# Attention and mixer kernel: scores with each head's q and k on its own half of the rows, and one group of four blocks in every other chunk transposed by DMA

## The chip, the cores and the metric

The kernel runs on one core of a Trainium2 chip. The metric is device time in microseconds (us). A core has TensorE (PE in the profile; PEld is its weight load), VectorE (DVE), ScalarE (ACT), GpSimd (POOL) and SyncE (SP). DMAs are issued from the queues of SP and ACT here.

## The reference, cut to what matters

Batch 4, 8 heads, 576 positions, head dimension 64, all in float32.

```python
scores = scale * np.matmul(q, k.transpose(0, 1, 3, 2))
...
h = np.maximum(x @ w1 + b1, 0.0)          # x: psi_rel / psi_i, 32 hidden
bias = h @ w2
scores = scores + bias.transpose(2, 0, 1)[None, :, :, :]
scores = scores - np.max(scores, axis=-1, keepdims=True)
attn = np.exp(scores)
attn = attn / (np.sum(attn, axis=-1, keepdims=True) + 1e-09)
return np.matmul(attn, v)
```

The result, reshaped to (4, 576, 512), goes through a mixer: a token step `u = x + (relu(x^T w_tok1) w_tok2)^T` and a channel step `u + relu(u w_ch1) w_ch2`.

## The kernel before

The work has three stages that overlap at their borders.

**Bias.** 36 blocks build the 8 x 576 x 576 bias. For each, ACT and DVE make four rectified tiles (lines 422 and 424), TensorE multiplies them with w2 into one of two PSUM tiles called `pair` (line 440, 16 instructions), `over` (line 446) scales them into one of four `eb` buffers, and `put` stores the buffer in DRAM (line 451, SP queue). Beside that, SP loads v once for its size (`sums`, line 465, eight loads) and the weights for their sizes (`meas`, line 303).

**Units.** A unit is one pair of heads of one batch entry; there are 16. It loads kT and qT (line 620, ACT queue) as tiles of 128 rows: rows 0 to 63 hold head dimensions for the two heads side by side (1152 columns), rows 64 to 127 hold the same again. A unit has five chunks of query rows, four of 128 and a last one of 64 rows per head that handles both heads at once. For each chunk:

- `scores` (line 653) multiplies q and k. In chunks 0 to 3 it is one step per head: two matrix products of 288 columns, one on rows 0 to 63 and one on rows 64 to 127, into the two banks of one `pair` tile. In the last chunk it is four products of 320 columns, two from each half of the rows, into the upper and the lower half of the partitions of one `pair` tile. A float32 product is two instructions in the profile.
- `biased` (line 657, DVE) adds the bias, takes the row maximum and writes the tile z; `top` (676 or 678) and `numer` (671, ACT) make the exponential in place.
- `flip` (line 690, TensorE) transposes groups of four blocks of 128 columns of z into a PSUM bank; `flip_hi` (693, ACT) and `flip_lo` (697, DVE) split them into two float16 parts in a `t2a` tile. FLIPS says how many groups each chunk turns this way: two in chunks 0 to 3, one in the last.
- The rest of z's columns, 128 of them in every chunk, is split into two float16 parts in a `p2` tile by `hi` (line 307) and `lo` (line 322, POOL) and transposed by DMA on the SP queue (`turn`, line 709) into one of two `t2` tiles.
- `back` (lines 733 to 735) multiplies the transposed attention with v in 30 products; the norm, the token mixer (783 to 785, 792 to 794) and a store follow at the end of a unit.

**Channel step.** Lines 955 to 957 and 985 to 987, with the decoding of its weights (lines 544 to 559) beside the units.

**Order.** Nothing is left to queues to decide: every step has a cost, a due time from the tables DUE, TICK and BASE, an engine choice from ON, and buffers that it takes and frees. `Plan.order` writes one fixed order of instructions per engine from these. A `scores` step of a head takes one of the two `pair` tiles and frees it after `biased`; a `turn` takes one of two `t2` tiles, which is free again after the `back` two chunks earlier. A DMA step on the SP queue is `D`, on the ACT queue `Q`, a DMA transposition on SP `X`.

Of the kernel before, what the change touches and what calls it, by code (L numbers as in the profile page):

```python
# [8 lines left out]
F32 = mybir.dt.float32  # L9
# [12 lines left out]
NF = 32  # L22
TAB = 1148
# [12 lines left out]
TICK = 2.39  # L36
BASE = 61.71
# [7 lines left out]
ON = {'top': {'V': (0.15, 0.74), 'A': (0.22, 0.08)},  # L45
      'dlo': {'V': (0.67, -2.69), 'P': (1.78, -2.0)},
      'norm': {'V': (0.35, -23.09), 'A': (0.88, 14.02)},
      'rect': {'A': 0.68, 'V': (0.45, -13.36)},
      'over': {'A': 0.65, 'V': (0.72, 6.22)},
      'vh': {'P': (0.7, -10.93), 'V': (0.4, 2.41), 'A': (0.6, -8.52)},  # L50
      'vl': {'P': (1.36, 16.26)},
      'hi': {'A': (1.05, -14.51), 'V': (0.67, 19.73)},
      'lo': {'P': (2.32, 8.15)}}
DUE = {'blk': 32.56,
       'blkn': 0.64,
       'rect': -60.12,
       'bmm': -130.42,
       'over': -7.68,
       'put': -27.47,
       'bl': -14.28,  # L60
       'bln': 15.14,
       'sums': -75.84,
       'sumsn': 0.81,
       'meas': -57.01,
       'measn': -1.94,
       'measw': 95.9,
       'measwn': 5.09,
       'amax': 57.87,
       'scales': 29.14,
       'scalet': -69.14,  # L70
       'scalec': -164.62,
       'fill': 232.3,
       'fill1': 251.05,
       'tok': 91.96,
       'tokn': 1.42,
       'dec1': 41.92,
       'dec2': -0.99,
       'dec3': -43.49,
       'dec4': 30.17,
       'dec5': 2.45,  # L80
       'load_k': -31.58,
       'load_q': 67.25,
       'load_v': -142.39,
       'prep_k': -55.55,
       'prep_kl': -22.13,
       'prep_q': 79.74,
       'prep_ql': 14.53,
       'prep_v': -118.61,
       'prep_vh': -0.88,
       'prep_vl': 145.08,  # L90
       'scores': 30.55,
       'biased': 82.97,
       'top': -4.71,
       'exp': -22.34,
       'hi': -110.65,
       'lo': -17.61,
       'flip': 33.53,
       'fliphi': 28.08,
       'flip2': 1.68,
       'fliplo': 9.58,  # L100
       'turn': -6.91,
       'back': -21.64,
       'norm': 85.56,
# [1003 lines left out]
```

## Time and profile before

| | |
|---|---|
| median of 3 runs | 718.59 us (713.29 to 719.01) |
| profiled execution | 719.23 us, of which the span is 717.4 us |
| mean granted TensorE clock over the span | 0.982 |
| PE busy | 663.8 us, 93% |
| DVE busy | 464.0 us, 65% |
| ACT busy | 377.4 us, 53% |
| POOL busy | 166.6 us, 23% |

The shares are means over stages with different limits, so the stages are read one by one. Busy times overlap: a matrix product's row lasts until its modelled end, while the next has already begun, so what a step costs TensorE is read from its start to the start of the next step. A queue's own rows (ACTq, SPq) are issues and waits, not computation.

### The profile page before, as it was taken

What the parts mean: (1) busy time and instruction counts of PE and PEld (TensorE: products, weight loads), DVE (VectorE), ACT (ScalarE), POOL (GpSimd) and SP (SyncE); (2) the same over time, 40 slices, a digit from 0 to 9 for tenths busy, and PEclk for the clock granted to TensorE, in tenths of its full rate; (3) what the DMA queues carried; (4) which work ended last, traced back from release to release, by engine and by line L of the source; (5) the groups of instructions that cost most, each with busy time, mean ns of one, the idle gap of its engine ahead of it and who ended that gap; (6) DMA issues with size and microseconds to landing.
All of it is one profiled execution on the core that took longest, in us unless ns stands there. A gap on an engine that the chain in (4) does not pass through costs nothing.

```text
span 717.4 us, 16724 instructions
## 1 busy us (share of the span) xinstructions
PE 663.8 (93%) x6612; PEld 396.6 (55%) x6612; DVE 464.0 (65%) x1122; ACT 377.4 (53%) x767; POOL 166.6 (23%) x228
## 2 busy tenths in 40 slices
PE   2775879999999999999979999999999999999997
PEld 1422346766767766777757676544444444446443
DVE  4598978987889998887887878479971022112110
ACT  1585878765877888867865853335531022012010
POOL 0102125232546543533322110003450000000000
PEclk9899999999999999999998999999999999999999
DMA  9978778897665586343552127967733120020021
GB/s 341 341 261 268 252 244 255 231 257 227 199 170 147 172 246 207 101 139 113 136 99 69 24 67 222 255 209 192 194 85 118 58 59 1 11 78 31 14 87 33
DMA packets 86815, 111.43 MB, mean 155 GB/s; under 512 B 46928, under 2 KB 56400, under 8 KB 86736
## 3 DMA queue, kind: packets, MB, share of 16 engines
q1 hardware_dynamic: 77232, 81.52, 39.3%
q10 hardware_dynamic: 9504, 28.84, 12.8%
q8 instruction: 52, 0.85, 0.5%
q14 instruction: 27, 0.22, 0.1%
HBM read 80.31 MB, written 20.05 MB: 140 GB/s over the span
## 4 chain that ended last, share of the span: by engine, by line
PE 74%; DVE 7%; DMA 7%; ACT 5%; issue 3%; POOL 2%; ACTq 0%; SPq 0%; POOLq 0%; DVEq 0%
PE pair L653 9%; PE bank L690 8%; PE bank L955 7%; PE bank L956 7%; PE bank L957 7%; PE bank L987 7%; PE bank L985 6%; PE bank L986 6%; PE bank L733 3%; DMA slots<-v 3%; PE pair L440 3%; PE bank L735 3%; PE bank L734 2%; DVE z L657 2%; DVE t2a L697 2%
## 5 line engine op out<-in xcount | busy, mean ns | idle before, releaser
L653 PE MATMUL pair<-kk,qq 64*128 64x288 f32 (+1 forms) x640 | 107.9, 458 | 8.0 <-DVE mx L657 5.0
L657 DVE CUSTOM_DVE_ANT_0 z<-pair,slots 128x576 f32<-128x576 f32 x144 | 108.0, 756 | 10.1 <-PE pair L653 9.5
L671 ACT ACTIVATE z<-z,mx 128x576 f32<-128x576 f32 x144 | 110.8, 774 | 5.8 <-POOL vl L322 1.9
L697 DVE TENSOR_TENSOR t2a<-bank,t2a 128x512 f16<-128x512 f32 x144 | 98.2, 686 | 21.5 <-ACT t2a L693 20.8
L693 ACT ACTIVATE t2a<-bank 128x512 f16<-128x512 f32 x144 | 84.5, 587 | 46.4 <-PE bank L690 41.9
L690 PE MATMUL bank<-id,z 128*128 128x128 f32 x576 | 95.4, 290 | 4.9 <-ACT z L671 4.8
L690 PEld LDWEIGHTS bank<-id,z 128*128 128x128 f32 x576 | 62.0, 143 | 36.8 <-issue 12.1
L996 DVE SCALAR_TENSOR_TENSOR o<-bank,crow,ur 128x512 f32<-128x512 f32 x18 | 13.5, 751 | 106.1 <-PE bank L987 106.1
L733 PE MATMUL bank<-vh,t2a 128*128 128x65 f16 (+1 forms) x704 | 76.9, 198 | 0.3 <-DVE x L767 0.2
L734 PE MATMUL bank<-vl,t2a 128*128 128x64 f16 (+1 forms) x704 | 76.2, 194 | 0.0
L733 PEld LDWEIGHTS <-t2a 128*128 128x128 f16 (+1 forms) x704 | 65.8, 100 | 18.6 <-issue 12.6
L735 PE MATMUL bank<-vh,t2a 128*128 128x65 f16 (+1 forms) x704 | 75.8, 195 | 0.0
L955 PE MATMUL bank<-slots 128*128 128x384 f16 (+1 forms) x192 | 67.8, 353 | 0.0
L956 PE MATMUL bank<-slots 128*128 128x384 f16 (+1 forms) x192 | 67.7, 353 | 0.0
L957 PE MATMUL bank<-slots 128*128 128x384 f16 (+1 forms) x192 | 67.7, 353 | 0.0
L734 PEld LDWEIGHTS <-t2a 128*128 128x128 f16 (+1 forms) x704 | 66.6, 102 | 0.5 <-issue 0.2
L735 PEld LDWEIGHTS <-t2a 128*128 128x128 f16 (+1 forms) x704 | 66.7, 101 | 0.0
L322 POOL TENSOR_TENSOR p<-z,p 128x128 f16<-128x128 f32 x80 | 35.4, 444 | 131.7 <-ACT p L307 109.0
L653 PEld LDWEIGHTS pair<-kk,qq 64*128 64x128 f32 (+1 forms) x640 | 43.4, 177 | 35.1 <-issue 14.4
L424 DVE TENSOR_SCALAR slots<-slots 128x576 f32<-128x576 f32 x108 | 53.1, 562 | 14.4 <-PE pair L440 14.3
L440 PE MATMUL pair<-slots 128*32 128x288 f32 x576 | 47.6, 448 | 14.6 <-ACT slots L446 14.2
L977 ACT ACTIVATE ur<-ur,sc 128x512 f32<-128x512 f32 x18 | 12.9, 719 | 83.1 <-DMA ur<-um 68.7
(173 smaller groups left out, 1410.4 us busy)
## 6 DMA issues: line engine op xcount, KB each, us to landing
raw<-wc SPq DMA_DIRECT2D x48, 512.0 KB, 4.3
bd<-slots SPq DMA_DIRECT2D x36, 288.0 KB, 3.6
kk<-kT ACTq DMA_DIRECT2D x16, 576.0 KB, 5.1
qq<-qT ACTq DMA_DIRECT2D x16, 576.0 KB, 6.2
slots<-bd SPq DMA_DIRECT2D x16, 576.0 KB, 4.7
tv<-v ACTq DMA_DIRECT2D x16, 320.0 KB, 3.8
slots<-v SPq DMA_DIRECT2D x8, 640.0 KB, 13.0
um<-x SPq DMA_DIRECT2D x16, 256.0 KB, 3.5
```

The costliest lines, as they stand in the source:

```text
L653: PE.matmul(out=o[:, n, 0:i], lhsT=qq[w, q0:q0 + m], rhs=kk[w, k0:k0 + i], start=True, stop=True)
L657: V.tensor_tensor_reduce(out=st["z"][z.i][:, o].rearrange("p (n j) -> p n j", n=2), in0=pairs[ph.i][:, :, 0:i], in1=(bias_m[hp][:, c, h, : ...
L671: A.activation(out=zz, in_=zz, func=ACTF.Exp, bias=mx_t[z.i][:, 2 + h:3 + h], scale=0.125)
L690: PE.transpose(banks[tb.i][:, n * 128:(n + 1) * 128], st["z"][z.i][:, 512 * i + n * 128:512 * i + (n + 1) * 128], id32)
L693: A.activation(out=st["t2a"][h.i][:, 0:4].rearrange("p n q -> p (n q)"), in_=banks[tb.i], func=ACTF.Copy)
L697: V.tensor_tensor(out=x[:, 512:1024], in0=banks[tb.i], in1=x[:, 0:512], op=ALU.subtract)
L733: PE.matmul(out=o, lhsT=lh, rhs=vh[:, n, 0:D + 1], start=(i == 0), stop=False)
L734: PE.matmul(out=ps[q, h, 0:D], lhsT=lh, rhs=vl[:, n, :], start=False, stop=False)
L735: PE.matmul(out=o, lhsT=ll, rhs=vh[:, n, 0:D + 1], start=False, stop=(i == 4))
L955: PE.matmul(out=ps[:, 0:n], lhsT=w[0][:, c], rhs=uh[:, c], start=(c == 0), stop=False)
L956: PE.matmul(out=ps[:, 0:n], lhsT=w[0][:, c], rhs=ul[:, c], start=False, stop=False)
L957: PE.matmul(out=ps[:, 0:n], lhsT=w[1][:, c], rhs=uh[:, c], start=False, stop=(c == 3))
```

## The change

q and k are laid out so that a head has rows of its own: head 0 on rows 0 to 63, head 1 on rows 64 to 127, each 576 columns. A load has half the bytes. `scores` is one step for both heads in chunks 0 to 3, four products of 288 columns that alternate between the halves of the rows, and it takes both `pair` tiles at once. In the last chunk each head multiplies from its own half, into its own half of the partitions, six products of 320, 256, 256, 320, 64 and 64 columns.

FLIPS goes from 22221 to 12121 per unit: chunks 0 and 2 turn one group by TensorE, and their DMA transposition has 640 columns in place of 128 (times two for the parts).

`put` goes from SP's queue to ACT's. Three kinds of loads are held back until a given `over` step is done: the later `sums` loads, the `meas` loads, and kT and qT of every unit but the first. The planner can hand out two buffers of one kind to a step. All numbers of DUE, ON, TICK and BASE are new, so the order on every engine is a new one.

```diff
+GATES = (4, 6, 14)
...
-TICK = 2.39
-BASE = 61.71
+TICK = 2.23
+BASE = 67.32
...
-FLIPS = "22221" * 16
+FLIPS = "12121" * 16
...
-QUEUE = {'put': 'D', 'bias': 'D', 'k': 'Q', 'q': 'Q', 'v': 'Q', 'out': 'D', 'ur': 'Q', 'sums': 'D', 'w2': 'D'}
...
+QUEUE = {'put': 'Q', 'bias': 'D', 'k': 'Q', 'q': 'Q', 'v': 'Q', 'out': 'D', 'ur': 'Q', 'sums': 'D', 'w2': 'D'}
...
                     for h in s.take:
-                        if not room[h.kind]:
+                        n = sum(o.kind == h.kind for o in s.take)
+                        if len(room[h.kind]) < n:
                             break
-                        t = max(t, min(room[h.kind])[0])
+                        t = max(t, sorted(room[h.kind])[n - 1][0])
...
-            st["kk"][i] = p.tile([128, PW], F32, name=f"kk{i}")
-            st["qq"][i] = p.tile([128, PW], F32, name=f"qq{i}")
+            st["kk"][i] = p.tile([128, S], F32, name=f"kk{i}")
+            st["qq"][i] = p.tile([128, S], F32, name=f"qq{i}")
...
+        def hold_back(s, n):
+
+            overs[n].next.append(s)
+            s.left += 1
+
+        for x, i in late:
+            if i >= GATES[0]:
+                hold_back(x, (i - GATES[0]) // 2)
...
-            x = add(wire("meas", 1.67 * n / 512), t, lambda e, h=h, w=w, n=n: load_words(e, st["raw"][h.i], w, n), take=[h])
+            x = add(wire("meas", 1.67 * n / 512), t, lambda e, h=h, w=w, n=n: load_words(e, st["raw"][h.i], w, n), after=[overs[GATES[1]]], take=[h])
...
-            lk = add(wire("k", 1.84), t0 + DUE["load_k"], load("kk", hk, kT), take=[hk])
-            lq = add(wire("q", 1.84), t0 + DUE["load_q"], load("qq", hq, qT), take=[hq])
+            early = [overs[min(GATES[2] * u, 35)]] if u else []
+            lk = add(wire("k", 1.0), t0 + DUE["load_k"], load("kk", hk, kT), after=early, take=[hk])
+            lq = add(wire("q", 1.0), t0 + DUE["load_q"], load("qq", hq, qT), after=early, take=[hq])
...
+                phs = [Hold("pair") for _ in range(2 if c < NCH else 1)]
+
+                def scores(e, c=c, phs=phs):
+
+                    kk, qq = st["kk"][hk.i], st["qq"][hq.i]
+                    if c < NCH:
+                        job = [(h, pairs[phs[h].i][:, n, 0:288], c * 128, 128, n * 288, 288) for n in range(2) for h in range(2)]
+                    else:
+                        ps = pairs[phs[0].i]
+                        job = [(0, ps[0:64, 0, 0:320], 512, 64, 0, 320), (1, ps[64:128, 0, 64:320], 512, 64, 0, 256),
+                               (0, ps[0:64, 1, 0:256], 512, 64, 320, 256), (1, ps[64:128, 1, 0:320], 512, 64, 256, 320),
+                               (0, ps[0:64, 1, 256:320], 512, 64, 512, 64), (1, ps[64:128, 0, 0:64], 512, 64, 0, 64)]
+                    for h, o, q0, m, k0, n in job:
+                        w = slice(64 * h, 64 * h + 64)
+                        PE.matmul(out=o, lhsT=qq[w, q0:q0 + m], rhs=kk[w, k0:k0 + n], start=True, stop=True)
+
+                lead = chain("scores", add({"T": 1.12 if c < NCH else 0.8}, t + DUE["scores"], scores, after=[*ready, *bias_in[hp, c]], take=[*phs, z], free=[hk, hq]))
+                for h, ph in enumerate(phs):
...
-                    s = add({"V": 0.68 if c < NCH else 0.75}, t + DUE["biased"], biased, after=[s, *tops], free=[ph])
+                    s = add({"V": 0.68 if c < NCH else 0.75}, t + DUE["biased"], biased, after=[lead, *tops], free=[ph])
...
-        return np.tile(x.reshape(NB, HP, 2, S, D).transpose(1, 0, 4, 2, 3).reshape(HP * NB, D, PW), (1, 2, 1))
+        return x.reshape(NB, HP, 2, S, D).transpose(1, 0, 2, 4, 3).reshape(HP * NB, 2 * D, S)
```

## Rows read from the trace of the kernel before

**Rows 1.** The profile's page, its part 1 (busy time, share of the span) and part 4 (the chain of work that ended last, by engine).

```profile
PE 663.8 (93%) x6612; PEld 396.6 (55%) x6612; DVE 464.0 (65%) x1122; ACT 377.4 (53%) x767; POOL 166.6 (23%) x228
...
PE 74%; DVE 7%; DMA 7%; ACT 5%; issue 3%; POOL 2%; ACTq 0%; SPq 0%; POOLq 0%; DVEq 0%
```

**Rows 2.** Busy time by stretch: the stretch in us, its length, then busy us and instructions of PE, PEld, DVE, ACT and POOL, the granted TensorE clock, the share of DMA, GB/s.

```profile
0.00:32.00 32.00, 15.71 (x179) 8.95 (x179) 14.62 (x41) 10.12 (x14) 2.08 (x16) 0.95 0.94 356
32.00:100.00 68.00, 49.74 (x569) 22.03 (x570) 58.87 (x134) 52.08 (x86) 13.59 (x16) 0.95 0.78 259
100.00:180.00 80.00, 74.15 (x991) 52.65 (x988) 67.74 (x178) 56.06 (x130) 25.85 (x41) 0.96 0.85 241
180.00:440.00 260.00, 252.45 (x3551) 183.88 (x3548) 218.59 (x557) 194.12 (x434) 99.80 (x132) 0.99 0.51 138
440.00:717.00 277.00, 271.79 (x1336) 129.14 (x1334) 104.14 (x215) 64.98 (x108) 25.24 (x24) 1.00 0.35 98
```

**Rows 3.** TensorE in order of time, 205.9 to 213 us: start, duration, line, operation. L653 is scores, L690 a flip, L733 to L735 a back.

```profile
205.90 0.66 PE L690 MATMUL bank<-id,z 128*128 128x128 f32 x4
206.49 0.77 PE L653 MATMUL pair<-kk,qq 64*64 64x320 f32 x8
207.19 0.66 PE L690 MATMUL bank<-id,z 128*128 128x128 f32 x4
207.68 0.19 PE L733 MATMUL bank<-vh,t2a 128*128 128x65 f16 x1
...
208.59 0.63 PE L690 MATMUL bank<-id,z 128*128 128x128 f32 x4
209.16 1.24 PE L653 MATMUL pair<-kk,qq 64*128 64x288 f32 x8
210.33 0.66 PE L690 MATMUL bank<-id,z 128*128 128x128 f32 x4
...
211.73 0.63 PE L690 MATMUL bank<-id,z 128*128 128x128 f32 x4
212.30 0.76 PE L653 MATMUL pair<-kk,qq 64*128 64x288 f32 x4
212.98 0.65 PE L690 MATMUL bank<-id,z 128*128 128x128 f32 x4
```

**Rows 4.** One line's instructions: all score products, and the token mixer's first line of its second part (ten instructions a unit): duration in ns least, median and most, then the starts of the first and the last.

```profile
L653 PE MATMUL pair<-kk,qq x640: 402/430/846, 52.7 to 420.3; 64*128 64x288 f32 x128, 64*64 64x320 f32 x32
...
L792 PE MATMUL bank<-hh,wt2h x160: 218/219/245, 131.6 to 442.6; 128*128 128x128 f16 x128, 128*64 128x128 f16 x32
```

**Rows 5.** Groups of instructions by line and shape: count, busy us, mean ns of one, idle time of the engine before them and what ended it.

```profile
L697 DVE TENSOR_TENSOR t2a<-bank,t2a 128x512 f16<-128x512 f32 x144 | 98.2, 686 | 21.5 <-ACT t2a L693 20.8
L657 DVE CUSTOM_DVE_ANT_0 z<-pair,slots 128x576 f32<-128x576 f32 x128 | 95.2, 748 | 8.5 <-PE pair L653 7.9
L693 ACT ACTIVATE t2a<-bank 128x512 f16<-128x512 f32 x144 | 84.5, 587 | 46.4 <-PE bank L690 41.9 <-DVE m L297 2.7 <-PE pair L653 1.1
L322 POOL TENSOR_TENSOR p<-z,p 128x128 f16<-128x128 f32 x80 | 35.4, 444 | 131.7 <-ACT p L307 109.0 <-ACT mx L676 16.7 <-DVE t2a L697 2.4
L307 ACT ACTIVATE p<-z 128x128 f16<-128x128 f32 x80 | 24.1, 303 | 2.6 <-POOL vl L322 2.1 <-ACT z L671 0.2
L322 POOL TENSOR_TENSOR xl<-x,xh 128x640 f16<-128x640 f32 x16 | 22.4, 1403 | 18.8 <-ACT xh L307 17.0 <-DVE mx L657 1.7
L307 ACT ACTIVATE xh<-x 128x640 f16<-128x640 f32 x16 | 11.7, 728 | 1.7 <-DVE x L767 1.6
```

**Rows 6.** Waits over the whole span: engine and line, what it waited for, us in total, times, the longest.

```profile
PEld pair L653 <- DVE mx L657: 10.9, 21, 3.8
...
PE pair L653 <- DVE mx L657: 5.0, 5, 3.6
```

**Rows 7.** DMA transpositions on the SP queue: L709 are the turns of z (two blocks of 128 columns each), L930 those of the channel step (four blocks). For each the issue (ns least, median, most), and the time to landing; the idle time of TensorE that ended with a turn; the wait of the SP queue for a free `t2` tile.

```profile
L709 SPq DMA_TRANSPOSE t<-p x80: 1167/1183/3247, 74.5 to 424.5; - x80
...
DMA to landing us min/median/max: 2.3/3.5/7.3
...
  DMA t<-p: 3.8, 4
...
L930 SPq DMA_TRANSPOSE slots<-slots x14: 1189/1216/1262, 358.6 to 449.6; - x14
...
DMA to landing us min/median/max: 2.4/2.5/6.4
...
SPq L709 <- PE bank L735: 74.0, 44, 6.2
```

**Rows 8.** The ACT queue and the SP queue at the start, in order of time: start, duration, queue, line, what is issued; in brackets the idle time before and what ended it.

```profile
2.12 14.26 SPq L465 DMA_DIRECT2D slots<-v  x8
...
9.73 7.58 ACTq L620 DMA_DIRECT2D qq<-qT  x3
17.42 0.77 ACT L422 ACTIVATE slots<-slots 128x576 f32<-128x576 f32 x1 [9.42 <-DMA kk<-kT]
...
31.55 1.45 ACT L446 ACTIVATE slots<-pair,slots 128x576 f32<-128x576 f32 x2 [4.42 <-DMA bd<-slots]
...
51.52 0.33 ACTq L624 DMA_DIRECT2D tv<-v  x1
```

More of the change, by code (lines that the diff above doesn't have):

```diff
@@ L54 @@
[L54 to L103, printed above, removed]
-       'mix0': -81.74,
-       'mix1': 47.34,
-       'relu': -93.88,
-       'mix2': -76.85,
-       'mix2b': -112.19,
-       'store': 54.71,
-       'w1': 37.13,
-       'w1n': 10.89,
-       'U0': -31.54,
-       'U0n': -5.32,
-       'U1n': -19.8,
-       'U1': -24.21,
-       'U2': 119.12,
-       'Un': 2.81,
-       'U3': 70.25,
-       'U4': 239.53,
-       'u1': -72.38,
-       'u2': -109.02,
-       'u3': 38.26,
-       'u4': 11.51,
-       'u5': 43.28,
-       'G': 99.65,
-       'G0': 57.68,
-       'G0n': 9.07,
-       'g1': -13.11,
-       'g2': 69.77,
-       'ur': 192.47,
-       'w2m': 23.69,
-       'w2mn': 2.89}
@@ new lines @@
+DUE = {'blk': 45.47,
+       'blkn': 0.37,
+       'rect': -103.97,
+       'bmm': -144.21,
+       'over': 16.18,
+       'put': -66.55,
+       'bl': -47.65,
+       'bln': 19.96,
+       'sums': -34.6,
+       'sumsn': 3.59,
+       'meas': -45.82,
+       'measn': -1.21,
+       'measw': 119.36,
+       'measwn': 4.97,
+       'amax': 112.97,
+       'scales': 100.93,
+       'scalet': -60.32,
+       'scalec': -217.57,
+       'fill': 223.82,
+       'fill1': 133.27,
+       'tok': 93.96,
+       'tokn': 4.05,
+       'dec1': 42.2,
+       'dec2': 35.45,
+       'dec3': -61.37,
+       'dec4': 32.74,
+       'dec5': 17.41,
+       'load_k': 0.68,
+       'load_q': 58.77,
+       'load_v': -127.05,
+       'prep_k': -87.23,
+       'prep_kl': -137.01,
+       'prep_q': 147.7,
+       'prep_ql': 18.38,
+       'prep_v': -172.66,
+       'prep_vh': -9.25,
+       'prep_vl': 157.67,
+       'scores': 34.55,
+       'biased': 81.29,
+       'top': 49.2,
+       'exp': -64.36,
+       'hi': -89.6,
+       'lo': -24.61,
+       'flip': 41.05,
+       'fliphi': 30.35,
+       'flip2': -7.08,
+       'fliplo': 40.47,
+       'turn': -12.01,
+       'back': 21.74,
+       'norm': 96.61,
+       'mix0': -106.16,
+       'mix1': 120.95,
+       'relu': -39.77,
+       'mix2': -117.22,
+       'mix2b': -216.31,
+       'store': 39.81,
+       'w1': 122.52,
+       'w1n': 16.06,
+       'U0': 24.71,
+       'U0n': -8.99,
+       'U1n': -17.52,
+       'U1': -65.65,
+       'U2': 159.58,
+       'Un': 1.74,
+       'U3': 37.55,
+       'U4': 228.93,
+       'u1': -130.89,
+       'u2': -119.65,
+       'u3': 84.5,
+       'u4': 6.97,
+       'u5': 88.69,
+       'G': 128.85,
+       'G0': 111.72,
+       'G0n': 8.72,
+       'g1': -54.42,
+       'g2': 111.4,
+       'ur': 165.46,
+       'w2m': -20.18,
+       'w2mn': 8.73}
@@ L458, in attention_mixer @@
                 m2 = big.tile([128, 32], F32, name="m2")
-                last = None
+                last, late = None, []
                 vh_ = Hold("bank")
@@ L660, in biased @@
                             scale=1.0, scalar=-3e38, op0=ALU.add, op1=ALU.max, accum_out=mx_t[z.i][:, h:h + 1])
-                    s = lead = chain("scores", add({"T": 0.6 if c < NCH else 0.66}, t + DUE["scores"], scores, after=[*ready, *bias_in[hp, c], lead if h else None], take=[ph, z] if h == 0 else [ph], free=[hk, hq]))
-                    s = add({"V": 0.68 if c < NCH else 0.75}, t + DUE["biased"], biased, after=[s, *tops], free=[ph])
+                    s = add({"V": 0.68 if c < NCH else 0.75}, t + DUE["biased"], biased, after=[lead, *tops], free=[ph])
                     last_use.setdefault(hp, []).append(s)
```

38 lines of the change are left out of this document (14 added, 24 removed).

## The prediction

> **What bounds it now.** Read the stages first [rows 2]: from 180 to 440 us, where the units run, TensorE is busy 252.5 of 260 us, from 440 on it is the only engine with much to do, and before 100 it waits for others (15.7 of 32 us, 49.7 of 68). The means over the span hide this: DVE's 65% [rows 1] is 218.6 of 260 us in the units, so it stands close behind. The chain that ended last is TensorE for 74% [rows 1]. In the units a step that leaves TensorE is therefore worth its time, so long as DVE doesn't take over; at the start only what DMA, ACT or DVE hold up counts. The channel step doesn't change: it begins earlier or later by what the units win or lose. The sum goes against the profiled execution, 719.2 us, of which 1.8 lie outside the span; it is 0.6 above the median of 718.6.
>
> **Flips taken away.** In order of time [rows 3], a flip followed by a back takes 0.49 us from start to start (207.19 to 207.68). Chunks 0 and 2 of 16 units lose one each: 32 x 0.49 = 15.7 us of TensorE. With each go a 587 ns ACTIVATE and a 686 ns TENSOR_TENSOR [rows 5]: 32 x 0.587 = 18.8 us of ACT, 32 x 0.686 = 22.0 us of DVE.
>
> **Scores joined.** A step of one head costs 0.68 us when it stands alone (212.30 to 212.98), two neighbours 1.17 (209.16 to 210.33): joining saves 2 x 0.68 - 1.17 = 0.19. The flip ahead also takes 0.57 to 0.59 before scores and 0.49 before a back, another 0.09 for each beginning [rows 3]. Between the first and last score products [rows 4] I count 128 runs of them without another step between; 96 are of one head alone, so most pairs are apart today. Afterwards there are at most five a unit, 80. So 48 x 0.28 = 13.4 us are saved.
>
> **The last chunk.** Its four products of 320 columns take 0.70 us together (206.49 to 207.19). The added pair of 288 in the run of two heads took 1.17 - 0.68 = 0.49, or 1.7 ns a column for two products side by side. Two by two, 2 x 320 columns would need 1.09 and the 0.19 of a run's end, 1.28; so today all four run at once [rows 3]. After the change a head has only its own half, and 640 columns pass there one product after another: I take 1.28, which costs 16 x 0.58 = 9.3 us. The bounds are 0.70 (nothing) and no overlap of the halves at all, 2 x 1.09 + 0.19 = 2.37, or 26.7 us. TensorE's sum: -15.7 - 13.4 + 9.3 = -19.8 us.
>
> **The wide part.** In 32 chunks `hi` and `lo` take 640 columns in place of 128. On ACT 728 ns for 303, on POOL 1403 for 444 [rows 5]: 13.6 us more for ACT, which still gains 5; 30.7 more for POOL, busy 99.8 of 260 [rows 2], so covered. If DVE gets `hi` instead, its nearest row (748 ns for 576 columns) bounds that at 24 us, and its gain is gone. The issue of a transposition is flat, 1183 ns for two blocks and 1216 for four [rows 7]; SP's in-order queue is held no longer by ten, as far as these show, so stores and weight loads behind a turn wait as now. Landing was 3.5 us for two blocks in the busy part and 2.5 for four later [rows 7], so eight more blocks cost between nothing and, at the longest narrow landing, 3.8; I take 5 us in all, near the median. A turn may start when the back two chunks earlier frees its tile. A unit lasts (442.6 - 131.6) / 15 = 20.7 us [rows 4], a chunk 4.1; after the change about 3.9, so the landing has 2 x 3.9 less the back's 0.9 (207.68 to 208.59 [rows 3]), or 6.9 us. Five fits, and today's narrow ones stop TensorE four times for 3.8 us in all [rows 7]. Cost: nothing, while a landing stays under 6.9.
>
> **The start.** ACT stands idle 9.42 us behind six loads of k and q that it issues, the last three held 7.58 us while SP's eight loads of v occupy the rings, and 4.42 us more for a bias store to leave [rows 8]. Halved loads, held back for units 1 and 2, and sums held back take aim at just these: at most 13.8 us. Against it, 36 stores move to ACT's in-order queue; at the 0.33 us of an issue there [rows 8] that is up to 12 us, and the rectified tiles and exponentials behind a store wait with it. SP's queue is freer by as much. From 32 to 100 DVE is the fuller engine (58.9 of 68, ACT 52.1 [rows 2]), so neither end comes out whole. I take -3, bounds -10 and +8. The halved bytes later on lie beside work (DMA at 0.51 [rows 2]) and count nothing, and neither do the holds on later k and q.
>
> **What comes back.** With 20 us less, DVE, ACT and the pair of PSUM tiles (below) are nearer to TensorE. DVE's 218.6 of 260 falls by about 15 while the stage loses some 13: from 84 to 82%, hardly more room than now. I let a quarter of the 19.8 be lost in new gaps: -14.9. Forecast: 719.2 - 14.9 - 3 = 701 us, by itself 690 to 709.
>
> **Rivals.** (1) *The two `pair` tiles become the wait.* A joined step needs both, so between its scores and the next both `biased` must pass: 1.17 + 2 x 0.75 + some 0.3 of handing over = 3.0 of the chunk's 3.9 us. TensorE waits on that row 10.9 us already on its weight side, up to 3.8 at once [rows 6]; against it, these are at most 26 waits among 128 runs. If each of 64 joined steps waits 0.3 us, 19 us: 701 + 19 less the 5 I gave back already = 715.
>
> (2) *The last chunk goes one half at a time*, so the change doesn't give what its layout says: both heads write one PSUM bank at once from different halves of the rows, which no row shows (today the halves use different banks). 26.7 in place of 9.3: 701 + 17.4 = 718, no change. The Trainium skill speaks for this rival (TensorEngine Tiling (Array Packing), Restrictions and Gotchas: row tiles must not access one bank at the same time), though its page PSUM — Partial Sum Buffer (PSUM bank collisions raise a hardware error) narrows that to the same quadrant of partitions, and here the heads write different partitions; no run here shows either yet.
>
> (3) *Slower: the wide turn is late.* Its place is the wait of `back` for the landing, its price what the landing exceeds 6.9 us by, 32 times; `back` is fixed in TensorE's order, so all behind it waits. For it: SP already waits 74.0 us in 44 turns for a free tile, so turns start late as it is; the longest narrow landing was 7.3 [rows 7], and `hi` and `lo` add 1.4 us ahead. Against it: the four-block landings. Slower by 1% is 726; from 719.2 - 19.8 - 3 = 696.4 that takes 30 us, or 0.9 a turn, a mean landing of 7.8. At 1.2 each, 38 us, it is 734. The Trainium skill has a rule that would bring this about (VectorE: DVE Perf Modes, The three transpose paths): a 128x128 block costs 1309 ns by DMA and 390 on TensorE, so use TensorE where PSUM will do. By it, as an estimate, eight blocks add 10.5 us and the landing of 14 misses by 7, over 200 us in all. The trace disagrees: four blocks landed in a median of 2.5 us, and a flip's four took 0.49 in a row [rows 3, 7].
>
> **Chances.** A measurement of this kernel tells about 1% from no change, here 711.4 to 725.8. Forecast 0.60; rival 1 0.16; rival 2 0.07; rival 3 0.13; 0.04 for a start that wins its full 10 and a stage that loses nothing (719.2 - 19.8 - 10 = 689). The first and last are faster, with a quarter of rival 1: 0.67. Rivals 2 and most of 1 are no change, with a little of the forecast: 0.19. Slower 0.14. The range 688 to 719 reaches from that best case over rivals 1 and 2, and leaves rival 3 out, with what overshoots either end.
>
> **What would show it.** Right: 64 joined scores of 8 instructions at about 1.17 us, 16 last ones of 12 near 1.28, TensorE's work before the channel step down by some 20 us, its wait for turns under 10 us, and ACT without the 9.4 us hole. Wrong: joined runs that wait on `biased` (rival 1), last chunks of 2.4 us (2), idle time of TensorE before L733 that ends with a turn and landings over 7 us (3), a bias stage that ends later than now because ACT's stores hold it (the start's sign). A weight decode that comes too late for the channel step, by the new due times, would show as TensorE idle after the units; I have no row that prices it.

## The result: 1% slower, where 2.5% faster was forecast

The changed kernel takes 723.1 us (median of 10 runs, 720.7 to 733.2), the kernel before 715.0 in the runs beside it (712.4 to 719.0). The ratio is 1.0101, with a 95% interval of [1.0073, 1.013]. The forecast was 701 us, its range 688 to 719. The two profiled executions stand closer, 721.1 against 719.2, since the one of before is 4.2 us above its kernel's median and the one of after 2.0 below. What the traces show side by side is therefore some 6 us kinder to the change than the medians are.

The page of the changed kernel, parts 1 and 4, as [rows 1]:

```profile
PE 658.5 (92%) x6548; PEld 409.9 (57%) x6548; DVE 441.1 (61%) x1069; ACT 378.7 (53%) x743; POOL 214.7 (30%) x254
...
PE 70%; DVE 9%; DMA 7%; ACT 6%; issue 4%; POOL 2%; ACTq 1%; SPq 0%; DVEq 0%; POOLq 0%
```

Busy time by stretch of the changed kernel, columns as in [rows 2]:

```profile
0.00:32.00 32.00, 19.28 (x253) 9.11 (x254) 21.53 (x51) 18.27 (x25) 3.60 (x17) 1.00 0.91 338
32.00:100.00 68.00, 47.46 (x450) 19.78 (x446) 47.50 (x117) 41.80 (x64) 11.40 (x12) 0.80 0.68 237
100.00:180.00 80.00, 71.72 (x979) 55.43 (x978) 65.34 (x164) 63.42 (x143) 42.23 (x55) 1.00 0.92 223
180.00:440.00 260.00, 246.36 (x3528) 195.16 (x3527) 203.13 (x520) 188.64 (x403) 132.05 (x143) 0.97 0.63 147
440.00:717.00 277.00, 273.70 (x1348) 130.39 (x1346) 103.56 (x221) 66.58 (x110) 25.47 (x28) 1.00 0.34 98
```

TensorE, DVE and ACT have less to do between 180 and 440 us, and yet the stretch holds no more units: the last token mix starts at 440.9 us in both traces. The 1.9 us by which the profiled executions differ lie behind it, in the channel step: the new order leaves 516 of its first products (`bank<-slots`) for after the last mix, the old one 504. TensorE idles there for 1.0 us, as before, so a late weight decode is not it. TensorE's busy time fell from 252.5 to 246.4 of 260, DVE's from 218.6 to 203.1. That is idle time, not gain. From 32 to 100 us the granted clock fell from 0.95 to 0.80.

Groups of the changed kernel (count, busy us, mean ns | idle before) and its DMA issues (count, KB each, us to landing), to be held against [rows 5]:

```profile
L669 PE MATMUL pair<-kk,qq 64*128 64x288 f32 (+2 forms) x704 | 116.6, 417 | 6.7 <-DVE mx L675 5.7
L324 POOL TENSOR_TENSOR p<-z,p 128x128 f16<-128x128 f32 (+1 forms) x80 | 67.6, 848 | 87.9 <-ACT p L309 82.3
L714 DVE TENSOR_TENSOR t2a<-bank,t2a 128x512 f16<-128x512 f32 x112 | 76.1, 686 | 25.9 <-ACT t2a L710 25.0
...
bd<-slots ACTq DMA_DIRECT2D x36, 288.0 KB, 4.7
...
kk<-kT ACTq DMA_DIRECT2D x16, 288.0 KB, 3.4
qq<-qT ACTq DMA_DIRECT2D x16, 288.0 KB, 4.6
```

The change did what it says: 32 flips fewer (112 subtractions for 144), 32 wide `lo` steps on POOL, halved loads, the stores on ACT. I counted TensorE's steps from start to start over the whole span, in both timelines. Flips went from 92.9 to 68.5 us, scores from 103.5 to 116.9, backs from 83.2 to 89.1. Together, waits included, that is 5.1 us less, where the forecast had 19.8. Idle time of TensorE, most of which lies in these steps, rose from 13.4 to 21.4 us between 100 and 430.

**The extra score time is waiting.** TensorE, and then DVE, of the changed kernel around one joined step (start, duration, line, operation, [idle before and what ended it]; L669 is scores, L675 `biased`, L557 a step of the weight decode):

```profile
279.12 0.75 PE L669 MATMUL pair<-kk,qq 64*128 64x288 f32 x2 [1.07 <-DVE mx L675]
280.66 1.63 PE L669 MATMUL pair<-kk,qq 64*128 64x288 f32 x6 [0.79 <-DVE mx L675]
```

```profile
278.31 0.75 DVE L675 CUSTOM_DVE_ANT_0 z<-pair,slots 128x576 f32<-128x576 f32 x1
...
278.98 0.95 DVE L557 TENSOR_SCALAR dc<-raw 128x512 int32<-128x512 int32 x1
279.85 0.74 DVE L675 CUSTOM_DVE_ANT_0 z<-pair,slots 128x576 f32<-128x576 f32 x1
```

The first head's tile comes free at about 279.0 and its first product starts. The second head's `biased` stands in DVE's order behind a decode step, so the other three products (six instructions) start 1.54 us later, inside the step. An undisturbed joined step takes 1.17 us, as forecast; the 59 after 100 us take 1.45 in the mean, up to 3.11. The difference is 0.28 a step, 16.8 us in all. Of these, 14.6 us lie between the products of one step, in 27 of the 59 steps; by the program only the second `pair` tile can be waited for there.

### The profile page after: what moved, and what is told of

It is laid out like the page before. It is cut to its first block, busy times and chain, and to the rows that moved or that the text cites. A ratio compares the mean times of both kernels' runs of the same rounds, so it can differ in the third digit from the quotient of the medians.

```text
span 719.3 us, 16478 instructions
## 1 busy us (share of the span) xinstructions
PE 658.5 (92%) x6548; PEld 409.9 (57%) x6548; DVE 441.1 (61%) x1069; ACT 378.7 (53%) x743; POOL 214.7 (30%) x254
## 3 DMA queue, kind: packets, MB, share of 16 engines
q10 hardware_dynamic: 14688, 30.02, 13.4%
## 4 chain that ended last, share of the span: by engine, by line
PE 70%; DVE 9%; DMA 7%; ACT 6%; issue 4%; POOL 2%; ACTq 1%; SPq 0%; DVEq 0%; POOLq 0%
PE pair L669 10%; PE bank L1003 6%; PE bank L1004 6%; PE bank L1002 6%; PE bank L972 6%; PE bank L974 6%; PE bank L973 6%; PE bank L707 4%; PE pair L442 3%; PE bank L750 3%; DVE z L675 2%; PE bank L752 2%; DVE t2a L714 2%; DMA bd<-slots 2%; PE bank L751 2%
## 5 line engine op out<-in xcount | busy, mean ns | idle before, releaser
L669 PE MATMUL pair<-kk,qq 64*128 64x288 f32 (+2 forms) x704 | 116.6, 417 | 6.7 <-DVE mx L675 5.7
L675 DVE CUSTOM_DVE_ANT_0 z<-pair,slots 128x576 f32<-128x576 f32 x144 | 107.2, 758 | 19.2 <-PE pair L669 14.9
L324 POOL TENSOR_TENSOR p<-z,p 128x128 f16<-128x128 f32 (+1 forms) x80 | 67.6, 848 | 87.9 <-ACT p L309 82.3
L714 DVE TENSOR_TENSOR t2a<-bank,t2a 128x512 f16<-128x512 f32 x112 | 76.1, 686 | 25.9 <-ACT t2a L710 25.0
L669 PEld LDWEIGHTS pair<-kk,qq 64*128 64x128 f32 (+1 forms) x704 | 68.2, 174 | 34.1 <-DVE mx L675 13.2
L710 ACT ACTIVATE t2a<-bank 128x512 f16<-128x512 f32 x112 | 65.2, 586 | 23.2 <-PE bank L707 19.1
L707 PE MATMUL bank<-id,z 128*128 128x128 f32 x448 | 71.2, 289 | 5.8 <-ACT z L688 4.4
L442 PE MATMUL pair<-slots 128*32 128x288 f32 x576 | 49.8, 467 | 20.6 <-ACT slots L448 19.8
L750 PE MATMUL bank<-vh,t2a 128*128 128x65 f16 (+1 forms) x544 | 61.4, 197 | 1.5 <-DVE x L784 0.9
L752 PE MATMUL bank<-vh,t2a 128*128 128x65 f16 (+1 forms) x544 | 60.4, 194 | 0.5 <-DVE t2a L714 0.5
L751 PE MATMUL bank<-vl,t2a 128*128 128x64 f16 (+1 forms) x544 | 60.8, 193 | 0.0
L707 PEld LDWEIGHTS bank<-id,z 128*128 128x128 f32 x448 | 49.2, 145 | 18.8 <-ACT z L688 7.9
L750 PEld LDWEIGHTS <-t2a 128*128 128x128 f16 (+1 forms) x544 | 50.9, 101 | 13.5 <-issue 9.5
L751 PEld LDWEIGHTS <-t2a 128*128 128x128 f16 (+1 forms) x544 | 51.5, 102 | 1.7 <-issue 1.4
L752 PEld LDWEIGHTS <-t2a 128*128 128x128 f16 (+1 forms) x544 | 51.6, 101 | 0.6 <-DVE t2a L714 0.6
```

Source lines behind the costliest of these rows:

```text
L442: PE.matmul(out=pairs[ph.i][NF * g:NF * g + NF, x, 0:288], lhsT=wf.rearrange("p g h -> p (g h)"), rhs=rect_t[4 * hs.i + g][:, 288 * x:288 ...
L669: PE.matmul(out=o, lhsT=qq[w, q0:q0 + m], rhs=kk[w, k0:k0 + n], start=True, stop=True)
L675: V.tensor_tensor_reduce(out=st["z"][z.i][:, o].rearrange("p (n j) -> p n j", n=2), in0=pairs[ph.i][:, :, 0:i], in1=(bias_m[hp][:, c, h, : ...
L707: PE.transpose(banks[tb.i][:, n * 128:(n + 1) * 128], st["z"][z.i][:, 512 * i + n * 128:512 * i + (n + 1) * 128], id32)
L714: V.tensor_tensor(out=x[:, 512:1024], in0=banks[tb.i], in1=x[:, 0:512], op=ALU.subtract)
L750: PE.matmul(out=o, lhsT=lh, rhs=vh[:, n, 0:D + 1], start=(i == 0), stop=False)
```

## Experiments

Where it says "order kept", every engine runs its instructions in the changed kernel's order (or that of before). Otherwise the planner wrote the order anew, with due times that were not fitted to that kernel; e14 shows what this alone can cost. e8 to e10, e12, e13 and e15 to e18 leave parts of the computation out.

**The start.** The changed kernel's ACT at the start (start, duration, queue or engine, [idle before]):

```profile
26.15 0.74 ACT L448 ACTIVATE slots<-pair,slots 128x576 f32<-128x576 f32 x1 [0.40 <-ACT slots L448]
26.93 0.33 ACTq L453 DMA_DIRECT2D bd<-slots  x1
27.30 0.78 ACT L424 ACTIVATE slots<-slots 128x576 f32<-128x576 f32 x1 [0.40 <-PE pair L442]
```

The 9.42 us hole of [rows 8] is gone, and the last bias product ends at 89.5 us, 93.8 before. But a store that ACT issues stands between two ACTIVATEs. Two `over` steps in a row begin 1.13 us apart with a store between them and 0.62 without (e1, medians of 11), so a store takes 0.5 us of ACT, more than the 0.33 of its issue. The first token mix starts at 136.8 us, 131.6 before [rows 4]: in these two traces the start lost 5.2 us, behind the bias stage.

e1, order kept, the 36 stores back on SP:

```diff
-ENG[e].dma_start(out=bd[c]...
+SP.dma_start(out=bd[c]...
```

> The changed kernel with its order on every engine kept; only the 36 bias stores are issued from SP's queue again, at the same places of the order. Theory A (two losses: at the start ACT stands about 0.40 us after each store it issues, and in the units a joined score step waits for the second pair tile): 30 such stands times 0.40 is 12 us of ACT at a stage where ACT and the PSUM pair set the pace, so the last bias product ends some 8 to 12 us earlier than 89.6 us, the time falls from 723 to 711-716 us, ratio to the kernel before 0.995 to 1.003. Theory B (the wide DMA transpositions come late and their POOL work delays the units): no change, 1.008 to 1.013. Theory C (the new order is worse in itself, whatever the queue): no change either.

718.2 us, ratio 1.0049 [1.0012, 1.0085]; first token mix at 133.8, last bias product's end at 88.7. By the ratios the queue of the stores costs about 0.5%, half of the whole loss, with an uncertainty of the same size. That is less than theory A expected, and the sign that it named, a bias stage that ends 8 to 12 us earlier, came out as 0.8. e5 below has the same queue and its first token mix at 138.0, so the 3 us of one trace show nothing by themselves.

e11, no holds (new order): the three `after=` conditions by `GATES` taken out.

> The changed kernel without the three holds (the late sums, the reads for the decode and the loads of k and q for later units may start as early as a buffer is free), with the order of work written anew by the planner for that. Theory A (the holds are worth little by themselves; what the start lost, it lost to joined steps and to stores issued by ACT): within 6 us of the changed kernel on either side, first token mix between 133 and 141 us. Rival B (the holds give back what the ACT-issued stores cost): slower by 6 to 14 us, with ACT or DVE idle behind loads before 60 us, as the 9.4 us in the kernel before. Rival C (the holds cost time, since they delay loads): faster by more than 6 us.

723.2 us, 1.0119 [1.0049, 1.019], first token mix at 133.2. The holds are worth nothing that can be measured.

e14, `QUEUE['put']` back to `'D'` and nothing else, so a new order for e1's queue:

> The changed kernel with the bias stores issued by SP again, as a whole computation and with the order of work written anew by the planner for that, so a candidate to beat both kernels. With the order kept this was worth 0.5%. Theory A (a new order uses SP's stores better: first token mix at 131 us or earlier): 708 to 714. Rival B (the due times were fitted to stores on ACT and a new order is no better): 716 to 726.

724.7 us, 1.0138 [1.0092, 1.0184], first token mix at 145.0. The same queue as e1 in another order costs 0.9% more: due times fitted to one queue need not suit another. The verdicts of e3, e4, e7 and e11 carry an error of that size.

**Wide turns and halved loads.** e3, before with `FLIPS = "12121" * 16` alone (new order):

> The kernel before with FLIPS 12121 alone, its own tables, planned anew: 32 groups by DMA in place of TensorE, nothing else. Theory A: the flips' part of the prediction holds, 15.7 us of TensorE go and most of it shows: ratio 0.98 to 0.99. Theory B: turns come late, ratio 1.00 to 1.02, with TensorE waiting on landings for more than 15 us. Theory C: says nothing of this, near 0.99.

750.7 us, 1.0478 [1.0406, 1.0549], the opposite of what theory A expected, and beyond theory B's range too. TensorE's idle time that ends with a turned tile, and the landings, of e3. This view adds the matrix products and their weight loads, so it counts each wait about twice; what the products alone waited is said behind each:

```profile
L709 SPq DMA_TRANSPOSE t<-p x80: 1167/1264/3204, 78.6 to 452.4; - x80
...
  DMA t<-p: 33.8, 15
...
DMA to landing us min/median/max: 2.3/4.0/14.4
```

The products alone waited 16.4 us. That is less than half of the 36 us that e3 lost; its order is new, and where the rest went is not shown. The same of the changed kernel, whose loads are half as large, with the products' own row below:

```profile
L726 SPq DMA_TRANSPOSE t<-p x80: 1167/1248/4249, 96.7 to 426.7; - x80
...
  DMA t<-p: 7.2, 6
...
DMA to landing us min/median/max: 2.3/3.7/8.5
...
PE bank L750 <- DMA t<-p: 3.4, 3, 1.5
```

e6, the changed kernel, order kept, each load of q and k twice as long, its second half unused:

```diff
-st["kk"][i] = p.tile([128, S], F32, name=f"kk{i}")
+st["kk"][i] = p.tile([128, PW], F32, name=f"kk{i}")
...
```

> The changed kernel, its order kept, but each load of k and q brings its 576 columns twice, 576 KB as before the change; the second copy is not used. Theory A2 (what the halved loads do is make room for the wide transpositions; e2 lost 14 us by that, not by its layout): 733 to 745 us, ratio 1.025 to 1.045, TensorE's idle time that ends with a turn from 7 to over 40 us (both of its rows), landings up to 10 us or more. Rival (e2 lost by its layout or by the order of its products): 722 to 726 us, ratio 1.008 to 1.015.

731.3 us, 1.0261 [1.0202, 1.032]. The stretch from 100 to 180 us of e6, and its turns:

```profile
100.00:180.00 80.00, 71.27 (x949) 55.05 (x949) 64.10 (x160) 61.97 (x138) 42.60 (x55) 0.97 0.94 240
```

```profile
  DMA t<-p: 12.8, 10
...
DMA to landing us min/median/max: 2.3/3.9/10.2
```

Bytes alone cost 1.6%. But the products' wait for turned tiles rose only from 3.4 to 6.1 us, far less than theory A2 had it, so most of what the bytes cost lies elsewhere and is not located here. e2 (order kept) also puts back the old layout, 576 KB a load, head after head inside the step and the old last chunk:

> The changed kernel with its order kept, a joined score step still takes both pair tiles, but q and k lie as before (both heads side by side, twice): head 0's two products come first and need the first pair tile alone, and the last chunk has four products again. Theory A: the joined step (1.45 us from start to next start on the mean, 1.17 without waits) begins up to half a step earlier where it waits for the second tile, and the last chunk goes from 1.23 to 0.70 us (16 x 0.53 = 8.5 us of TensorE): 5 to 12 us faster than the changed kernel, ratio 0.994 to 1.003, although k and q are loaded twice. Theory B: less than 3 us of gain, ratio 1.006 or more. Theory C: only the last chunk's part, 1.00 to 1.005.

727 to 741 us in four runs, too scattered for a ratio. Its score steps became shorter (97.2 us from 100 to 430 us, 109.3 in the changed kernel), some 8 us of it by the old last chunk, and TensorE waited for turns instead, the products alone for 27.4 us:

```profile
  DMA t<-p: 56.6, 30
...
DMA to landing us min/median/max: 2.3/4.0/15.7
```

So theory A missed: the old layout brings no gain with the bytes it needs. At equal bytes e2 stands about where e6 does (729.7 to 738.2 us); too few runs to say more.

e8, the changed kernel, order kept, each turn cut to two blocks:

```diff
-SP.dma_start_transpose(out=...[:, 0:wn // 64], in_=...[:, 0:2 * wn])
+SP.dma_start_transpose(out=...[:, 0:2], in_=...[:, 0:256])
```

> The changed kernel, its order kept, with each DMA transposition cut to two blocks (256 columns); the other eight blocks of the wide ones are left as zeros, so that part of the attention is left out. hi and lo still run at full width. Theory A: in the changed kernel the wide turns are mostly in time (TensorE's idle time that ends with a turn is 7.2 us over both its rows, half of it real), so 2 to 6 us are gained, ratio 1.002 to 1.008. Theory B: the wide transfers hold the units up also through other loads; 10 us or more, ratio under 0.997.

722.4 us, 1.0117 [1.0066, 1.0168]: no gain, not even theory A's small one. With halved loads the width of a turn costs nothing measurable; with full ones more turns are late (e6, e2).

**Scores joined.** e4, before with the new loads and joined scores and the old flips (new order):

> The kernel before with the scores' part alone (a half of the rows for each head, one step for both heads, both pair tiles taken at once, half the bytes), its own tables, planned anew. Theory A: the joined steps wait for the second tile by about 0.3 us each (19 us), which eats the 13.4 us of fewer switches, and the last chunk adds 8.5: ratio 1.01 to 1.03, and units interleave less with the bias stage. Theory B: 4 to 5 us faster as the prediction's sum says, ratio 0.99 to 1.00. Theory C: near 1.00.

729.7 us, 1.0197 [1.0142, 1.0251]. Its first scores start at 69.0 us (52.7 before, 89.6 in the changed kernel): a step that needs both `pair` tiles fits badly between bias products, which take the same tiles. Yet its first token mix comes at 130.4 us, no later than before; e4 lost its time after that, 330 us from the first mix to the last one's end against 311, and why is open.

e5, e1 with each second `biased` moved right behind the first in DVE's order:

```diff
+for s in [s for s in line if getattr(s, "twin", None)]:
+    line.remove(s)
+    line.insert(line.index(s.twin) + 1, s)
```

> As e1 (bias stores from SP), and on DVE the second head's biased stands right behind the first's, with everything else in the order kept; today up to eight other DVE instructions stand between them while the next joined score step waits for the second pair tile. Theory A (the wait for the second tile is what eats the saved switches, about 17 us over the joined steps): joined steps fall from 1.45 to about 1.25 us on the mean, the time from 718 to 706-713 us, ratio to the kernel before 0.990 to 0.998. Theory B (turns by DMA and POOL set the pace): no gain, 1.003 or more. Theory D (DVE is the bound in the units, so whatever is put first, something else waits): within 2 us of e1, 1.003 to 1.007, with new waits of TensorE on other DVE work of about the size of those that went.

718.6 us, 1.0052 [1.0012, 1.0092], as e1. The joined steps did shorten (scores 103.8 us from 100 to 430 us for 108.6 in e1), and the backs took most of it up (92.6 for 89.5, with idle time at 23.0 for 20.2; the products' wait for turned tiles alone went from 3.5 to 6.3). The wait moved; it did not go.

e7, e1 with `FLIPS = "22221" * 16` (new order):

> e1 with FLIPS 22221 again, planned anew with the changed kernel's tables: the scores' part without the flips' part. Theory A: TensorE has 15.7 us more of flips and DVE 22 us more; slower than e1 by 8 to 16 us, ratio 1.015 to 1.03. Theory B: faster than e1, ratio under 1.003, since the wide turns are gone.

719.4 us, 1.0083 [1.0053, 1.0112], between the two expectations. Putting 14 us of flips back on TensorE costs 0.3% against e1, or nothing, as the intervals overlap. Its first token mix comes at 130.0 us, though its first scores, like the changed kernel's, start at 90.0.

**What sets the pace.** e7 asks whether TensorE's time still counts. The next eight runs keep the order of either kernel and take work away. e9 and e10, `flip_lo` cut to 64 columns:

```diff
-V.tensor_tensor(out=x[:, 512:1024], in0=banks[tb.i], in1=x[:, 0:512], ...
+V.tensor_tensor(out=x[:, 512:576], in0=banks[tb.i][:, 0:64], in1=x[:, 0:64], ...
```

> The kernel before, its order of work kept on every engine; the subtraction behind each flip (L696, 144 of them, 686 ns each) writes 64 of 512 columns, and `back` reads the high half where it read the low one. The low parts of the flipped exponentials are left out. DVE loses about 144 x 0.45 = 65 us of work, TensorE nothing. Theory A (DVE that reaches the second `biased` late hides the gain of the change): the kernel before, whose scores go head after head, was held by DVE less; it falls by 4 to 10 us, to a ratio of 0.986 to 0.995. Rival B (TensorE's own sum sets the time of both kernels, DVE of neither): within 3 us of the kernel before, and the same for the changed one. Rival C (DVE bounds both alike): 0.96 to 0.98 for both.

> The changed kernel, its order of work kept on every engine, with the same relief: 112 subtractions of 64 in place of 512 columns, the low parts of the flipped exponentials left out. DVE loses about 112 x 0.45 = 50 us. Theory A: the joined steps no longer wait inside for the second pair tile; their mean between 100 and 430 us falls from 1.45 to 1.25 us or less, TensorE's gaps there from 21 to 13 us or less, and the kernel falls by 15 to 25 us, to 698 to 708, well under the relieved kernel before (ratio between the two 0.975 to 0.99). Rival B: nothing moves by more than 3 us. Rival C: both relieved kernels fall alike, and the changed one stays about 1% above the other. If the steps fall and the time does not, the wait is at another place that the windows will name.

e12 and e13, 32 flips cut to one block, in chunks 0 and 2 in e12 and, as the changed kernel has no second flip there, in 1 and 3 in e13:

```diff
-for n in range(4):
+for n in range(1 if i == 1 and c in (0, 2) else 4):
```

> The kernel before, its order of work kept on every engine: the second flip of chunks 0 and 2 of each unit (32 of them, those that the change takes away) transposes one block in place of four, and the copy and the subtraction behind it take 128 columns in place of 512; `back` reads that block four times, so three blocks of each of these groups are left out of the attention. No transfer becomes wider. TensorE loses about 32 x 0.36 = 11.5 us, ACT 32 x 0.4 = 13, DVE 32 x 0.45 = 14. Theory A, the premise of the prediction (in the units a step that leaves TensorE is worth its time): 702 to 706 against some 714, a ratio of 0.983 to 0.988. Rival B (TensorE waits at the next step for what it has gained): 711 to 716, a ratio of 0.997 or more, with gaps or longer steps of TensorE in the place of the flips. The relief of DVE by 65 us without any for TensorE gave 0.9937, so what goes beyond that is TensorE's.

> The changed kernel, its order of work kept, with the same cut in the second flip of chunks 1 and 3 of each unit (again 32 flips, about 11.5 us of TensorE, three blocks of each group left out of the attention). Theory A (TensorE still sets the pace there): its ratio falls from 1.010 to 0.992 to 0.997. Rival B (the joined steps, the turned tiles and the copies set the pace now, and TensorE's time is no longer the price): a ratio of 1.003 or more. If the kernel before gains and this one does not, the change took what there was to take from TensorE and met the next limit.

e15 and e18, loads of q and k cut from the fourth unit on; e16 is e10 and e13 together, e17 all three:

```diff
+w = S if u < 3 else 64
-ENG[e].dma_start(out=st[tiles][h.i], in_=x[order_of[u]])
+ENG[e].dma_start(out=st[tiles][h.i][:, 0:w], in_=x[order_of[u]][:, 0:w])
```

> The changed kernel, its order of work kept: from the fourth unit on, each load of q and k brings 64 of 576 columns (32 KB in place of 288), so the scores of those units use what an earlier unit left; 26 x 256 KB = 6.7 MB less to read. Theory A (transfers that share the 16 DMA engines set the changed kernel's pace, as the 8 to 11 us lost with doubled loads suggest): its ratio to the kernel before falls from 1.010 to 1.000 or less. Rival B (at 288 KB the loads have already stopped mattering; a chain of hand-overs between the engines sets the pace): 1.006 or more.

> The changed kernel, order kept, with the cuts of e10 and e13 together: one block in place of four in the second flip of chunks 1 and 3, and subtractions of 64 columns; low parts and three blocks of each of these groups are left out. Theory A (TensorE and DVE hold the changed kernel up by turns, so that relieving one alone shows the other): both together give 10 us or more, a ratio of 0.997 or less. Rival B (neither sets the pace): no more than the relief of DVE alone, 1.003 to 1.010.

> The changed kernel, order kept, with the cuts of e15 and e16 together. Theory A (transfers set the pace, and once they are out of the way TensorE's time counts again): at least 10 us under e15's own, a ratio of 0.985 or less. Rival B (the chain of hand-overs sets the pace whatever is relieved): 0.998 or more.

> The kernel before, order kept, with its loads of q and k cut to 64 of 1152 columns from the fourth unit on, 26 x 544 KB = 14.1 MB less to read. If TensorE sets its pace, as its gain from fewer flips says, it moves by less than 3 us (0.996 to 1.004). If transfers held it up too, it falls by 5 us or more, and the halved loads should have been worth that to the change by themselves.

All ratios are to the kernel before:

| work taken away, order kept | kernel before | changed kernel |
|---|---|---|
| nothing | 1 | 1.0101 [1.0073, 1.013] |
| fewer flips (e12, e13) | 0.9869 [0.9826, 0.9913] | 1.0099 [1.0065, 1.0134] |
| DVE relieved (e9, e10) | 0.9937 [0.9904, 0.997] | 1.0056 [1.002, 1.0092] |
| both (e16) | not run | 0.9993 [0.9962, 1.0024] |
| light loads (e18, e15) | 0.9994 [0.9965, 1.0024] | 1.013 [1.0088, 1.0172] |
| all three (e17) | not run | 0.9926 [0.9895, 0.9957] |

In the kernel before, the very flips that the change takes away are worth 1.3%, 9.4 us for some 12 us of TensorE, when nothing else changes. (12 us of DVE go with them, but e9 took 58 from DVE and gained 4.5.) In the changed kernel a cut of the same size is worth nothing that can be measured; the intervals leave room for some 0.4%. e13's trace shows where it goes: from 100 to 430 us the flips lost 12.0 us and the backs took 8.7 more, and TensorE's idle time rose by 7.0. Turned tiles, of e12 first (no line for a wait, so none), then of e13:

```profile
L711 SPq DMA_TRANSPOSE t<-p x80: 1167/1183/2271, 72.2 to 408.1; - x80
its engine sat idle before it (us, times) until:
...
DMA to landing us min/median/max: 2.3/3.4/9.0
```

```profile
  DMA t<-p: 19.5, 14
...
DMA to landing us min/median/max: 2.3/3.8/10.4
...
PE bank L752 <- DMA t<-p: 9.3, 7, 3.2
```

Busy time from 180 to 440 us, e12 and then e13:

```profile
180.00:440.00 260.00, 253.64 (x3525) 181.37 (x3526) 215.16 (x565) 185.69 (x431) 99.45 (x130) 1.00 0.53 148
```

```profile
180.00:440.00 260.00, 242.03 (x3499) 189.54 (x3497) 197.59 (x529) 181.79 (x405) 131.98 (x143) 0.97 0.64 151
```

With less to do, TensorE of the kernel before stays as full as it was (253.6 of 260), so the work behind it comes sooner; TensorE of the changed kernel empties (242.0) and sits in front of turned tiles, 3.4 us of the products' time becoming 9.3, nearly all by which its idle time rose. DVE's relief alone brings 0.45% there. Both together bring 1.1%. That is more than the two alone add up to (0.5%), but not by more than the intervals together, and e16 stays just above the 0.997 that theory A had set. e10's theory A, 15 to 25 us from DVE's relief, missed: both kernels fell alike. Light loads bring nothing alone to either kernel. e17 falls between its two expectations; the 0.7% by which it stands under e16 rests on intervals that just part, and e15 alone gained nothing that would explain it.

So no single relief that was tried frees the changed kernel. Its TensorE waits by turns for `biased`, for the exponentials and for turned tiles (5.7, 4.4 and 3.4 us of the products' idle time), and where one wait was shortened (e5, e13) another grew.

## Why the prediction was wrong

**Flips taken away: right in size, wrong in worth.** Flips fell by 24.4 us where 15.7 and the 4.3 ahead of scores were counted, the rest being waits that stood in the flips. e12 confirms the premise that a step which leaves TensorE is worth its time, for the kernel before. It stopped holding once the rest of the change was in (e13). So the premise "a step that leaves TensorE is therefore worth its time, so long as DVE doesn't take over" failed: DVE did not take over (78% busy), and the time still wasn't won.

**Scores joined: the step right, the saving not.** 1.17 us is the step's floor, but its mean is 1.45. The 0.09 of each beginning was saved: flips ahead of scores fell from 109 to 52. A little comes back where a back stands ahead of scores, 23 times for 10: it takes 1.00 us there and 0.92 ahead of a flip, 1 us in all. The other 5 us by which the backs grew are idle time that lies in them (8.5 us, 3.6 before). What ate the 13.4 us is the 16.8 of waiting.

**The last chunk: right.** It takes 1.23 us, 1.28 were forecast. Rival 2 is out: both heads write one PSUM bank from different halves of the rows and run side by side. By the rule of the Trainium skill (TensorEngine Tiling (Array Packing), Restrictions and Gotchas) they must not; the narrower one of the Trainium skill (PSUM — Partial Sum Buffer, PSUM bank collisions raise a hardware error), by which two row tiles collide within one bank and one quadrant of the partitions, is the one that these 16 steps agree with.

**The wide part: nothing, but on a condition that I had dropped.** The median landing of all turns moved from 3.5 to 3.7 us. Told apart by their `lo` steps, the 32 wide ones land in a median of 4.9 us, the 48 narrow ones in 3.4, so the 5 us that I took were right. Five wide ones pass 6.9 (up to 8.5), TensorE's products wait 3.4 us for turns in all, and e8 gains nothing, so rival 3 did not come about. (The 3.8 us in four stops that I read for the kernel before counted each stop twice; it is 1.8 in two.) By the figure of the Trainium skill beside it (VectorE: DVE Perf Modes, The three transpose paths), 1309 ns a block, ten blocks would take 13 us, as an estimate; the 4.9 us of this trace disagree. A term put at nothing wrongly is "the halved bytes later on lie beside work and count nothing", though it isn't what made the kernel slower. With full loads turns land after up to 14.4 us in e3, and e6 loses 1.6%. The mean DMA share of 0.51 hid that from 100 to 180 us it is 0.85 already [rows 2].

**The start: wrong sign.** -3 us were forecast, +5.2 came, by one trace each. The bias stage itself did end 4.3 us earlier, so the loss lies between its end and the first token mix. The stores on ACT cost about 0.5% by e1, at 0.5 us each more than the 0.33 that I counted. That joined steps start 37 us later I hadn't seen, but e4 and e7, whose first scores are also late, have their first mix at 130.4 and 130.0. It is the wide part that goes with a late first mix: all six kernels with two flips in chunks 0 and 2 have it between 129.1 and 131.6 us, the fourteen with one flip there between 133.2 and 145.0, e3 among them, with the old scores and the old queue. By which path stays open, since e8's short turns don't bring it back (136.9). A low clock may be part of it in the trace of the changed kernel (last section).

**What comes back: the step that decides.** "I let a quarter of the 19.8 be lost in new gaps." In the traces 14.7 of the 19.8 are lost, mostly as waits in the steps that remain. I compared DVE's mean share before and after, 84 and 82% (it is 78), as though room were spread evenly. A joined step asks for two `biased` results at once, and a back for wide turns and flips both; such meetings are lost when one side is late, and a mean share doesn't show that. Rival 1 had the mechanism and its price right (0.3 us a step forecast, 0.28 found), with a chance of 0.16 that was far too small for a wait of 3.0 us in a chunk of 3.9. Its 715, with the start at +5.2 in place of -3, is 723; that this is the median is luck, since the sum goes against a trace of 719.2 and the trace of the changed kernel has 721.1. But the `pair` tiles are only where the wait shows first: e5 took it from there and it came up at the backs.

No run of a whole computation beat the kernel before; e1 came nearest. One rival is left: that the order written for the changed kernel, and not its joined steps and wide turns, makes these waits. A new order alone moved the time by 0.9% (e14), so it could. Whether a layout like this with due times fitted to e1's queue, or with a third `pair` tile, would win was not tried.

## What to carry to other kernels

Before you count a step that leaves the fullest engine, ask what the step behind it needs and when that is ready; a cheap test is to cut the same work from the kernel as it is (e12) and from the changed one (e13). Joining two steps saves their switch but makes one step wait for the later of two inputs, so price it by how far apart the producers stand in their engine's order. Read the share of DMA in the stage where a latency matters, and price a store on an engine's queue by how far it moves that engine's next instruction, not by its issue time alone. When a view sums the waits for a tile, see whether it counts one wait on two rows.

## What the runs showed of the hardware

- Two fp32 products from different halves of the rows run side by side even where both write one PSUM bank, in different partitions: 2 x 640 columns in 1.23 us.
- A DMA transposition of ten blocks is issued in a median of 1.39 us and lands in 4.9, one of two blocks in 1.18 and 3.4 (changed kernel). With loads of 576 KB in the kernel the longest landings of turns were 10.2 (e6), 14.4 (e3) and 15.7 us (e2), with 288 KB 8.5 (changed kernel) to 11.1 (e10).
- A store that ACT issues between two of its ACTIVATEs moves the second by 0.5 us (1.13 from start to start, 0.62 in e1), its issue being 0.33.
- In the changed kernel the granted clock is 0.80 from 32 to 100 us and 0.50, the level of 1.2 GHz, from 96 to 100. TensorE had been busy 5.5 us of the 8 from 84 to 92, waiting mostly for `over` (ACT). Scores at that level take twice the 1.17 us, and the steps from 92.5 to 100.2 some 4 us more than at 2.4 GHz:

```profile
92.49 2.55 PE L669 MATMUL pair<-kk,qq 64*128 64x288 f32 x8 [0.48 <-DVE mx L675]
96.01 2.29 PE L669 MATMUL pair<-kk,qq 64*128 64x288 f32 x8
```

- The start scatters: the first token mix of kernels with the changed kernel's order on every queue came at 136.8 us (changed), 137.6 (e13), 140.3 (e15) and 143.0 (e10), on different executions, so a start of one trace is good to a few us only. The low clock doesn't decide it: e15 is late though its first scores ran at a granted clock of 1.00.
